# The last expert's first layer reads its rows, or writes its bank, in interleaved orders of columns

## The chip, the cores and the metric

The kernel runs on one core of one Trainium2 chip. The metric is the device time of one execution in microseconds. Five engines work side by side: TensorE (PE, with its weight loads apart as PEld), VectorE (DVE), ScalarE (ACT), GpSimd (POOL) and SyncE (SP), which issues most transfers. SBUF is the memory that the engines read; PSUM holds matmul results, in banks of 512 float32 values per partition.

## What is computed

The first half is a retention layer: for every batch and head a state decays by a factor and takes in one outer product of key and value at each step, and the query reads it. Its result, 3072 rows of 512 values, goes through a mixture of eight experts of which each row uses one:

```python
logits = x @ w_gate
expert_idx = np.argmax(logits, axis=1)
...
for e in range(E):
    mask = expert_idx == e
    xe = x[mask]
    h = np.maximum(xe @ w1[e], 0.0)
    ye = h @ w2[e]
    out[mask] = gate_w[mask, None] * ye
```

w1 of an expert is 512 x 1024, w2 is 1024 x 512. Only the first layer, `h`, of one expert is touched by the change.

## The kernel before

The retention part takes the first third of the time: it makes the rows, chooses experts, and scatters the rows into regions of HBM by expert. Then the experts run one after another in a loop over `e` (in `moe_main`); the experts are sorted by their number of rows, and each place in that order has a fixed capacity, `CAPS = [128, 452, 424, 412, 400, 392, 360, 376]`. The last one, `e` = 7, has room for 376 rows.

An expert's rows lie turned in SBUF: `xs[e]` is a pair of tiles of 128 partitions x 4 slices (`kd`) x 452 columns, a column for each row of the expert. Every float32 operand is cut into a high and a low part (`xh` and `xl`, `whi` and `wlo`), and three products of parts stand for one product.

The first layer runs over eight blocks of features, `f` = 0 to 7. A block is 128 features, the partitions of one PSUM bank; the bank's columns are the expert's rows. It takes twelve matmuls (three products times four `kd`) into the bank `ph`, line 1193, and three banks go round. How many columns each matmul takes is set at run time: `columns` (line 986) compares the number of rows that the expert holds with three widths, for the last expert 360, 368 and 376, and branches to a copy of the twelve matmuls of that width. When a block is done, ScalarE takes the bank through a Relu into `hh` (line 1200, the high part) and VectorE subtracts to get `hl` (line 1201); both always cover the whole capacity, `cap`. After each block some small jobs follow, such as cutting weights (lines 147 and 148) and scattering results of the expert before (line 860 on GpSimd).

The second layer reads `hh` and `hl` of all eight blocks. For the last expert its rows come as the result's partitions, in three steps of up to 128 rows: line 1223 for two steps, and line 1041 for the last one, in two halves of 256 result columns, whose `rhs` is read in runs of 64 columns. Within a step the blocks are taken in order, three matmuls each. The result goes through VectorE (lines 1024 and 1047) and a scatter on GpSimd (line 860) to the output.

The order of the work is that of the code: the schedule is manual, each engine runs its instructions in the order written, and waits by semaphores.

Some other lines come up below. Line 410 sums logits in PSUM over four parts that lie 32 columns apart. Line 826 reads the 7 x 7 table `sel` turned, so each value is 7 values (28 bytes) behind the last, and line 798 reads the same table in order. Line 470 reads a bf16 table at steps of 8 values (16 bytes). Line 465 sums over a row in order. Line 501 writes single values into `xrow` at steps of 130 values (520 bytes).

## Time and profile before

| what | value |
|---|---|
| median of 3 runs | 379.49 us (379.46 to 383.19) |
| the profiled execution | 379.21 us |
| its span, first to last instruction | 377.4 us |
| TensorE busy | 370.0 us (98% of the span) |
| VectorE, ScalarE, GpSimd busy | 255.1, 140.6, 261.7 us |
| mean granted TensorE clock | 1.000 |

The profile is taken from one execution. Its times count from the first instruction. A busy TensorE is one that has a matmul in its pipeline: matmuls overlap, so a matmul's duration is longer than the time from its start to the next one's start, and it is starts that say how fast the stream goes.

## The change

For the last expert alone (`COMBED` = 7) a table gives each of the eight blocks an order of columns: `b` parts, runs of `c` columns, and whether the reading of x (`read`) or the writing of the bank (`write`) is interleaved. A reading with b = 2, c = 1 takes column 0, 188, 1, 189 and so on; one with b = 188, c = 1 takes every second column, then the others; with b = 2, c = 4 it takes four columns of the first half, four of the second, and so on. A writing with c = 4 or 2 puts runs of four or two alternately into the two halves of the bank's 376 columns. All twelve matmuls of a block use the same order. The evictions put the columns back into their natural order, so `hh` and `hl` and all behind them are as before; where c is above 1 an eviction is split into `b` = 2 pieces of 188 columns. The expert no longer branches by its number of rows: it always takes 376 columns.

```diff
+COMBED = 7
+COMBS = ((1, 1, 0, 0), (2, 1, 1, 0), (2, 4, 0, 1), (4, 1, 1, 0), (2, 2, 0, 1), (8, 1, 1, 0), (2, 4, 1, 0), (188, 1, 1, 0))
...
+                b, c, read, write = COMBS[f] if e == COMBED else (1, 1, 0, 0)
+                comb = lambda t, apart: (
+                    t if b == 1 else t.rearrange("p (b a c) -> p a b c" if apart else "p (a b c) -> p a b c", b=b, c=c))
...
-                            nc.tensor.matmul(out=ph[:, :w], lhsT=wparts[e, f // 4][a][:, kd, fo:fo + P],
-                                             rhs=x[:, kd, :w], start=(n == 0), stop=(n == 3 * KD - 1))
+                            nc.tensor.matmul(out=comb(ph[:, :w], write), lhsT=wparts[e, f // 4][a][:, kd, fo:fo + P],
+                                             rhs=comb(x[:, kd, :w], read), start=(n == 0), stop=(n == 3 * KD - 1))
...
-                columns(e, hidden)
+                if e == COMBED:
+                    hidden(cap)
+                else:
+                    columns(e, hidden)
...
-                nc.scalar.activation(out=hh[:, :cap], in_=ph[:, :cap], func=AF.Relu)
-                nc.vector.scalar_tensor_tensor(out=hl[:, :cap], in0=ph[:, :cap], scalar=0.0,
-                                               in1=hh[:, :cap].bitcast(F32), op0=ALU.max, op1=ALU.subtract)
+                piece = lambda t, apart, i: (comb(t, apart) if c == 1 else t.rearrange(
+                    "p (b a c) -> p b a c" if apart else "p (a b c) -> p b a c", b=b, c=c)[:, i])
+                for i in range(b if c > 1 else 1):
+                    hhi, hli, phi = [piece(t[:, :cap], apart, i) for t, apart in ((hh, read), (hl, read), (ph, write))]
+                    nc.scalar.activation(out=hhi, in_=phi, func=AF.Relu)
+                    nc.vector.scalar_tensor_tensor(out=hli, in0=phi, scalar=0.0, in1=hhi.bitcast(F32),
+                                                   op0=ALU.max, op1=ALU.subtract)
```

On TensorE, at the start of the last expert's first layer, there stood before, for block 0 (bank `ph_2198`), the three widths behind two branches:

```order
L986 COMPARE_AND_BRANCH
L1193 MATMUL ph_2198<-xh,whi 128x360 x4
L1193 MATMUL ph_2198<-xh,wlo 128x360 x4
L1193 MATMUL ph_2198<-xl,whi 128x360 x4
L986 UNCONDITIONAL_BRANCH
L986 COMPARE_AND_BRANCH
L1193 MATMUL ph_2198<-xh,whi 128x368 x4
L1193 MATMUL ph_2198<-xh,wlo 128x368 x4
L1193 MATMUL ph_2198<-xl,whi 128x368 x4
L986 UNCONDITIONAL_BRANCH
L1193 MATMUL ph_2198<-xh,whi 128x376 x4
```

In the changed kernel (line 1193 is 1199 there) there stand blocks 1, 2, 3 and 4 one behind the other, without a branch; the shape shown is that of the bank's side:

```order
L1199 MATMUL ph_2199<-xh,whi 128x376 x4
L1199 MATMUL ph_2199<-xh,wlo 128x376 x4
L1199 MATMUL ph_2199<-xl,whi 128x376 x4
L1199 MATMUL ph_2197<-xh,whi 128x47x2x4 x4
L1199 MATMUL ph_2197<-xh,wlo 128x47x2x4 x4
L1199 MATMUL ph_2197<-xl,whi 128x47x2x4 x4
L1199 MATMUL ph_2198<-xh,whi 128x376 x4
L1199 MATMUL ph_2198<-xh,wlo 128x376 x4
L1199 MATMUL ph_2198<-xl,whi 128x376 x4
L1199 MATMUL ph_2199<-xh,whi 128x94x2x2 x4
L1199 MATMUL ph_2199<-xh,wlo 128x94x2x2 x4
L1199 MATMUL ph_2199<-xl,whi 128x94x2x2 x4
```

The number of matmuls is the same, twelve a block; their width and the order of their columns are new. On ScalarE the same stretch read before, from the eviction of block 0 on (in brackets the semaphores, by the engine that raises them, that an instruction waits for):

```order
L1200 ACTIVATE hh<-ph_2198 128x376 [waits PE_49,Activation_49]
L147 CAST whi<-raw 128x1024 [waits DMAHW2_49,Activation_49]
L986 UNCONDITIONAL_BRANCH
L1200 ACTIVATE hh<-ph_2199 128x376 [waits PE_49,Activation_49]
L147 CAST whi<-raw 128x1024
L1200 ACTIVATE hh<-ph_2197 128x376 [waits PE_49,Activation_49]
```

and after, from the eviction of block 1 to that of block 7:

```order
L1213 ACTIVATE hh<-ph_2199 128x188x2 [waits PE_49,Activation_49]
L149 CAST whi<-raw 128x1024
L1213 ACTIVATE hh<-ph_2197 128x47x4 [waits PE_49,Activation_49]
L1213 ACTIVATE hh<-ph_2197 128x47x4 [waits DVE_49]
L1213 ACTIVATE hh<-ph_2198 128x94x4 [waits PE_49,Activation_49]
L1213 ACTIVATE hh<-ph_2199 128x94x2 [waits PE_49,Activation_49]
L1213 ACTIVATE hh<-ph_2199 128x94x2 [waits DVE_49]
L1213 ACTIVATE hh<-ph_2197 128x47x8 [waits PE_49,Activation_49]
L1213 ACTIVATE hh<-ph_2198 128x188 [waits PE_49,Activation_49]
L1213 ACTIVATE hh<-ph_2198 128x188 [waits DVE_49]
L1213 ACTIVATE hh<-ph_2199 128x2x188 [waits PE_49,Activation_49]
```

Blocks 2, 4 and 6 have two evictions, the second of which waits for VectorE. VectorE's side, line 1214 there, is cut in the same way. GpSimd's and SyncE's instructions keep their order.

## Rows read from the trace of the kernel before

**Rows 1.** The page: busy us (share of the span) and instructions of each engine.

```profile
PE 370.0 (98%) x3279; PEld 348.4 (92%) x3279; DVE 255.1 (68%) x499; ACT 140.6 (37%) x252; POOL 261.7 (69%) x277
```

**Rows 2.** Busy time by stage: stretch, its us, each engine's busy us, clock, DMA.

```profile
339.37:355.20 15.83, 15.83 (x98) 15.83 (x97) 8.60 (x13) 5.26 (x9) 12.86 (x14) 1.00 0.09 28
355.20:372.00 16.80, 16.80 (x97) 14.62 (x96) 2.53 (x4) 0.48 (x1) 12.23 (x15) 1.00 0.17 55
```

**Rows 3.** Who waited for whom from 338 us on: total us, times, longest.

```profile
ACT hh L1200 <- PE ph L1193: 12.6, 8, 4.0
DVE yo L1024 <- PE py L1223: 9.3, 2, 4.8
```

**Rows 4.** GpSimd's timeline at the end: start, us, what, idle before and its releaser.

```profile
372.98 1.01 POOL L860 DMA_INDIRECT out<-yo,pair  x1 [1.80 <-DVE yo L1047]
```

**Rows 5.** TensorE's timeline, last expert's first layer, four matmuls a row.

```profile
339.37 0.82 PE L1193 MATMUL ph<-xh,whi 128*128 128x360 f32 x4
340.03 0.82 PE L1193 MATMUL ph<-xh,wlo 128*128 128x360 f32 x4
```

**Rows 6.** The same of an expert with 392 columns, five blocks apart.

```profile
240.10 0.88 PE L1193 MATMUL ph<-xh,whi 128*128 128x392 f32 x4
...
250.80 0.52 PE L1193 MATMUL ph<-xh,whi 128*128 128x392 f32 x2
```

**Rows 7.** TensorE's timeline, last second layer: 512 columns, then runs of 64.

```profile
355.20 0.40 PE L1223 MATMUL py<-whi,hh 128*128 128x512 f32 x1
...
356.83 0.40 PE L1223 MATMUL py<-wlo,hh 128*128 128x512 f32 x1
...
366.33 0.28 PE L1041 MATMUL py<-whi,hh 128*120 128x256 f32 x1
...
367.51 0.28 PE L1041 MATMUL py<-wlo,hh 128*120 128x256 f32 x1
```

**Rows 8.** Groups by shape: count | busy us, mean ns of one | idle before.

```profile
L1200 ACT ACTIVATE hh<-ph 128x452 fp32r<-128x452 f32 x8 | 4.4, 548 | 9.1 <-PE ph L1193 9.0
L1200 ACT ACTIVATE hh<-ph 128x376 fp32r<-128x376 f32 x8 | 3.9, 486 | 12.6 <-PE ph L1193 12.6
L501 ACT COPY xrow<-GW 128x8 f32<-128x8 f32 x4 | 0.8, 205 | 6.0 <-DVE GW L496 6.0
L501 ACT COPY xrow<-GW 128x24 f32<-128x24 f32 x2 | 0.5, 239 | 5.1 <-DVE GW L496 5.1
L1201 DVE SCALAR_TENSOR_TENSOR hl<-ph,hh 128x452 fp32r<-128x452 f32 x8 | 5.0, 625 | 2.7 <-ACT hh L1200 2.1
L1201 DVE SCALAR_TENSOR_TENSOR hl<-ph,hh 128x376 fp32r<-128x376 f32 x8 | 4.4, 547 | 7.1 <-ACT hh L1200 7.0
L410 DVE TENSOR_REDUCE lg<-lp 128x16 f32<-128x64 f32 x8 | 1.8, 223 | 6.7 <-PE lp L404 6.7
L465 DVE TENSOR_REDUCE KEY<-rk 128x2 int32<-128x16 f32 x4 | 0.7, 170 | 0.1
L470 DVE TENSOR_REDUCE tot<-EA 128x8 bf16<-128x16 bf16 x3 | 0.5, 151 | 0.0
L465 DVE TENSOR_REDUCE KEY<-rk 128x6 int32<-128x48 f32 x2 | 0.4, 203 | 0.1
L470 DVE TENSOR_REDUCE tot<-EA 128x8 bf16<-128x48 bf16 x2 | 0.4, 200 | 0.0
L826 DVE TENSOR_TENSOR se<-sel,cs 128x49 f32<-128x49 f32 x1 | 0.3, 252 | 0.0
L798 DVE TENSOR_TENSOR se<-sel,others 128x49 f32<-128x49 f32 x1 | 0.2, 202 | 0.0
```

**Rows 9.** Evictions of the last expert: timelines of ScalarE and VectorE.

```profile
341.61 0.49 ACT L1200 ACTIVATE hh<-ph 128x376 fp32r<-128x376 f32 x1 [4.05 <-PE ph L1193]
342.13 0.55 DVE L1201 SCALAR_TENSOR_TENSOR hl<-ph,hh 128x376 fp32r<-128x376 f32 x1
355.92 0.55 DVE L1201 SCALAR_TENSOR_TENSOR hl<-ph,hh 128x376 fp32r<-128x376 f32 x1 [1.43 <-ACT hh L1200]
```

## What I expected of the change before it ran

> **What bounds the kernel now.** I read the page first. TensorE is busy 370.0 of 377.4 us [rows 1]. So whatever lengthens TensorE's stream lengthens the run, if the engine is not waiting there. The table by stage says where the change lies: the last expert's first layer runs from 339.37 to 355.20, 15.83 us with TensorE busy for 15.83 of them and a clock of 1.00, and the last second layer follows without a gap, 16.80 of 16.80 us [rows 2]. TensorE is not among the waiters of that stretch: the longest waits are ScalarE's for a bank from TensorE (12.6 us) and VectorE's for TensorE (9.3 us) [rows 3]. Behind TensorE's last matmul only one VectorE step, one GpSimd scatter and its landing are left: GpSimd waited 1.80 us for VectorE before the last scatter at 372.98 [rows 4]. So a microsecond more on TensorE between 339 and 355 is a microsecond more in the time.

> The profiled execution took 379.21 us with a span of 377.4; the sum below is made on 379.21, which is 0.28 under the median of 379.49.

> **The change part by part.**

> *No arms any more.* Before, each block takes the narrowest of 360, 368 and 376 columns that holds the expert's rows, and every matmul of the trace took 360 [rows 5]; after, all 96 take 376. A block of twelve lasts 15.83/8 = 1.979 us at 360 columns [rows 2]. At 392 columns five blocks run from 240.10 to 250.80, 10.70/5 = 2.140 us [rows 6]. That is 0.161 us for 32 columns, so 0.080 for 16: a block of 376 takes 2.059 us, and eight cost 8 x 0.080 = **0.64 us**. The branch that goes away gives nothing back: 1.979 us over twelve is 165 ns a matmul, and four matmuls of one kind within a block take 0.66 us, 165 ns too [rows 5].

> *Reads of x in another order.* Blocks 1, 3 and 5 read x one column at a time from 2, 4 or 8 places of the row, so neighbours in the stream lie 752, 376 or 188 bytes apart. Block 6 takes runs of four columns (16 bytes) from two places, block 7 every second column (8 bytes apart). No TensorE row of before steps through its moving operand by single columns. The nearest, the last rows' matmuls, jump after each run of 64 columns: ten of them from 366.33 to 367.51, 118 ns for 256 columns, 0.46 ns each, against (356.83 - 355.20)/7 = 233 ns for 512 in a row, also 0.46 [rows 7]. So a jump as such is free, and the lower bound for all five blocks is nothing (a gain is excluded: no matmul streams fewer columns). The upper bound comes from other engines that step through SBUF element by element. VectorE's product of 49 values reads `sel` in order in 202 ns (L798), and turned, at 28 bytes a step, in 252 (L826): 50 ns more over 49 values, 1.0 ns each, and a value in order costs (203 - 170)/32 = 1.03 ns (L465): the price doubles. At 16 bytes a step (L470) it is (200 - 151)/32 = 1.53 ns, half as much again. ScalarE's writes at 520 bytes a step (L501) cost (239 - 205)/16 = 2.1 ns, against (548 - 486)/76 = 0.82 in order (L1200) [rows 8]. Three rows of two engines say that single four-byte elements, each far from the last, run at half rate or a little worse. I take half rate for TensorE in blocks 1, 3 and 5: each goes from 2.059 to 4.118 us, 3 x 2.059 = **6.18 us**. For runs of four (block 6) I take the row of jumps, nothing. For steps of 8 bytes (block 7) I take nothing too, since that lies nearer to stepping by 4 than to the 16 bytes that cost half; its bounds are 0 and 2.06 us.

> *Writes of the bank in another order.* Blocks 2 and 4 write runs of four and of two columns alternately into the two halves. No row shows TensorE writing so. VectorE's sum of 64 logits reads PSUM at 128 bytes a step in 223 ns (L410); at 1.03 ns a value from the 170 ns of 16 values (L465) 64 in order would be 219 [rows 8]. So a PSUM walk with gaps costs VectorE nothing, and I take 0 for TensorE's; the other bound is half rate, 2 x 2.059 = 4.12 us. [...]

> *Evictions.* They are as wide as before (376) and now step; those of blocks 2, 4 and 6 come in two pieces of 188, where ScalarE's second waits for VectorE's first, by the order above. Now one takes 486 ns on ScalarE and 547 on VectorE [rows 8]. The chain of block 0 runs from 341.61 to 342.13 + 0.55 = 342.68 [rows 9], and its bank is written again by block 3, at 339.37 + 3 x 1.979 = 345.31: 2.6 us of cover. Two pieces cost two more fixed parts: at 0.82 and (625 - 547)/76 = 1.03 ns a value, 188 take 332 and 353 ns, so two of each in series take 1.37 us against 1.03. A stepped eviction of block 1 at the dearest price of rows 8 takes 486 + 376 x 1.3 = 0.97 us on ScalarE and 547 + 376 x 1.0 = 0.92 on VectorE: 0.9 us more. Both stay under the cover, which grows as blocks get longer. Behind block 7 the second layer needs its result only at its 22nd matmul, 21 x 0.233 = 4.9 us on, and it is ready 1.3 us after the layer's end now [rows 7, 9]. So **0**; without that cover each of the seven would cost up to 0.9 us.

> *The tail.* GpSimd waits for VectorE, and VectorE for TensorE, before the last scatter [rows 3, 4]; a later TensorE moves them along: 0.

> Sum: 379.21 + 0.64 + 6.18 = **386.0 us**, 1.7% above the median.

> **The rivals.**

> *Stepped reads are free on TensorE.* Then only the columns are left: 379.21 + 0.64 = 379.9 us, not slower. [...] Against it: three rows that agree in direction. It decides if a block of 1, 3, 5 costs less than 1.1 us extra, for then the sum stays under 1% (383.3). A half price, as at 16 bytes (1.03 us a block), gives 382.9 and falls here.

> *Writes into the bank in runs are slow as well:* 386.0 + 4.12 = 390.1 us. For it nothing in a row; against it L410. [...] If only they are slow, 384.0.

> *Stepping by 8 bytes is slow as well:* 386.0 + 2.06 = 388.1 us.

> *TensorE pays the other engines' nanoseconds, not their ratio.* At 1.0 ns more for each of 376 columns, 36 matmuls pay 13.5 us: 379.85 + 13.5 = 393.4. For it: VectorE's and ScalarE's stepped prices, 2.1 ns, are alike though their rates in order differ. I hold it less likely, since TensorE takes 0.46 ns a column now, so it reads faster than either.

> *The evictions become the bound:* TensorE would show waits for a bank at blocks 3 to 7. The cover of 2.6 us against 0.9 speaks against it; chance next to nothing.

> **How the numbers follow.** Half rate in three blocks alone 0.43 (own range 385.0 to 386.6: the doubling taken as 0.95 to 1.05); free 0.24 and half price 0.08; with PSUM writes 0.13, of which 0.02 without the reads; with the 8-byte steps 0.06; the nanoseconds 0.06. The time forecast is the likeliest one's, 386.0. From 379.6 (free, less the 0.3 that executions differ) to 390.4 all is held but the last: about 0.9, and it could not end lower without leaving out a bound that no row closes. About 1% is what a measurement of this kernel can tell from no change. Slower by more: 0.43 + 0.13 + 0.06 + 0.06 = 0.68; within: 0.31; faster: 0.01, for nothing in the change shortens TensorE's stream.

> **What would show it.** In the changed profile the last first layer should last 15.83 + 6.82 = 22.7 us. The starts of TensorE's groups of four say which step was right: 0.69 us from group to group in blocks 0, 2, 4, 6 and 7, and 1.37 in blocks 1, 3 and 5. 0.69 everywhere makes the first rival right; 1.37 in blocks 2 and 4 the second, in block 7 the third; over 2 in blocks 1, 3, 5 the fourth. TensorE gaps before blocks 3 to 7 with ScalarE or VectorE as their end would show the evictions. The prediction is wrong above all if the moving operand goes through a path that does not care where the next column lies, or if 2, 4 and 8 places differ, which I have not priced.

## The result, and the profile of the changed kernel

| what | before | changed |
|---|---|---|
| median of 16 runs each | 379.48 us | 384.05 us |
| ratio, 95% interval | | 1.012 (1.0096 to 1.0144) |
| the last first layer on TensorE | 15.83 us [rows 2] | 20.58 us |
| the last second layer, to TensorE's end | 16.95 us | 16.98 us |

The changed kernel is slower by 4.6 us, a little over 1%; forecast were 386.0 us. A ratio leaves out the slowed-down executions, which the medians keep, so it is not exactly the quotient of two medians. The execution that was profiled first (388.28 us) lost 4.3 us ahead of the change, about places where TensorE was idle (0.58 us before 23.93, 1.90 before 98.17). The times of its other runs (at most 385.79) and a second profile of the same kernel do not show that loss, so all rows of the changed kernel are from the second profile (384.33 us, span 382.5). It reaches the layer at 339.64, where before it was 339.37 [rows 5].

The page's engines, as [rows 1]: TensorE has 5.0 us more, the others at most 1.8.

```profile
PE 375.0 (98%) x3279; PEld 349.9 (91%) x3279; DVE 256.9 (67%) x502; ACT 142.2 (37%) x255; POOL 260.6 (68%) x277
```

The two stages, as [rows 2], with the same columns (stretch, its length, then the engines' busy time, clock, DMA share and GB/s):

```profile
339.64:360.22 20.58, 20.58 (x98) 17.51 (x97) 10.14 (x16) 6.88 (x12) 15.64 (x19) 1.00 0.10 30
360.22:377.20 16.98, 16.98 (x97) 14.63 (x95) 2.53 (x4) 0.52 (x1) 8.00 (x10) 1.00 0.14 45
```

TensorE is busy in every microsecond of both, at a granted clock of 1.00: the 4.75 us are longer matmuls and no wait. Where they lie is read from starts. This is TensorE's timeline, as [rows 5] (start, us, what), with the first group of each of the eight blocks, the second group of block 0, and the first matmul of the second layer:

```profile
339.64 0.85 PE L1199 MATMUL ph<-xh,whi 128*128 128x376 f32 x4
340.33 0.85 PE L1199 MATMUL ph<-xh,wlo 128*128 128x376 f32 x4
...
341.70 0.80 PE L1199 MATMUL ph<-xh,whi 128*128 128x376 f32 x4
...
343.61 0.85 PE L1199 MATMUL ph<-xh,whi 128*128 128x376 f32 x4
...
345.68 0.96 PE L1199 MATMUL ph<-xh,whi 128*128 128x376 f32 x4
...
348.08 0.86 PE L1199 MATMUL ph<-xh,whi 128*128 128x376 f32 x4
...
350.15 1.47 PE L1199 MATMUL ph<-xh,whi 128*128 128x376 f32 x4
...
354.04 0.90 PE L1199 MATMUL ph<-xh,whi 128*128 128x376 f32 x4
...
356.23 1.50 PE L1199 MATMUL ph<-xh,whi 128*128 128x376 f32 x4
...
360.22 0.41 PE L1236 MATMUL py<-whi,hh 128*128 128x512 f32 x1
```

The difference of two starts is a block, and a twelfth of it a matmul:

| block | order | us | ns a matmul | forecast us |
|---|---|---|---|---|
| 0 | as it was | 2.06 | 172 | 2.06 |
| 1 | reads two places | 1.91 | 159 | 4.12 |
| 2 | writes runs of four | 2.07 | 172 | 2.06 |
| 3 | reads four places | 2.40 | 200 | 4.12 |
| 4 | writes runs of two | 2.07 | 172 | 2.06 |
| 5 | reads eight places | 3.89 | 324 | 4.12 |
| 6 | reads runs of four, two places | 2.19 | 182 | 2.06 |
| 7 | reads every second column | 3.99 | 332 | 2.06 |

The reads alone differ: two places are *faster* than columns in a row (159 ns against 172), four a little slower, eight nearly twice as slow, and so is every second column. Here more places also lie closer together; which of the two counts, the measuring kernels below tell apart.

The waits of that stretch, from 338 us on, as [rows 3] (total, times, longest):

```profile
ACT hh L1213 <- PE ph L1199: 14.0, 8, 4.1
...
POOL out L862 <- DVE yo L1049: 3.4, 2, 1.8
...
ACT hh L1213 <- DVE hl L1214: 1.7, 3, 0.9
```

No row has TensorE as the waiter. The new one, ScalarE for VectorE, three times, is the second pieces of blocks 2, 4 and 6. GpSimd's last wait is 1.8 us as in [rows 4], so the tail is what it was. The evictions, as [rows 9], on ScalarE in blocks 0, 1, 2 (two pieces), 5 and 7, and on VectorE in blocks 1 and 7:

```profile
341.96 0.48 ACT L1213 ACTIVATE hh<-ph 128x376 fp32r<-128x376 f32 x1 [4.13 <-PE ph L1199]
343.87 0.88 ACT L1213 ACTIVATE hh<-ph 128x376 fp32r<-128x376 f32 x1 [0.49 <-PE ph L1199]
345.94 0.33 ACT L1213 ACTIVATE hh<-ph 128x188 fp32r<-128x188 f32 x1 [0.33 <-PE ph L1199]
347.16 0.33 ACT L1213 ACTIVATE hh<-ph 128x188 fp32r<-128x188 f32 x1 [0.90 <-DVE hl L1214]
354.32 0.85 ACT L1213 ACTIVATE hh<-ph 128x376 fp32r<-128x376 f32 x1 [2.78 <-PE ph L1199]
360.50 0.52 ACT L1213 ACTIVATE hh<-ph 128x376 fp32r<-128x376 f32 x1 [2.93 <-PE ph L1199]
```

```profile
344.79 0.86 DVE L1214 SCALAR_TENSOR_TENSOR hl<-ph,hh 128x376 fp32r<-128x376 f32 x1
...
361.05 0.55 DVE L1214 SCALAR_TENSOR_TENSOR hl<-ph,hh 128x376 fp32r<-128x376 f32 x1 [3.10 <-ACT hh L1213]
```

ScalarE, which reads the bank in order and writes `hh` at the interleaved places, takes 1.8 times as long for single columns at far places (0.88 us for 0.48). VectorE, which reads `hh` and writes `hl` there, takes 1.6 times as long (0.86 for 0.55). Two places or eight are alike, and every second column costs next to nothing (0.52 and 0.55). TensorE's order is another: it pays for the second column (332 ns a matmul for 172) and not for the two places (159).

## The experiments

Every kernel was run beside runs of the kernel before on the same chip, and a ratio is to those.

### The changed kernel again

No edit; it asks whether the loss ahead of the change belongs to it.

> The changed kernel once more, unedited, beside runs of before on the same chip. Its first profile lost 4.3 us ahead of the change, at 22 and 95 us. If that has nothing to do with the change, a second profile reaches the last expert's first layer near 339.3, as before did, spends 20.6 us in it again, and the time is about 384.0; if it belongs to the change, the loss comes back.

Measured: 383.95 us against 379.03, ratio 1.012 (1.0086 to 1.0153). The early loss was gone (the layer begins at 339.64, in the first profile at 343.66); the layer itself lasted 20.58 us in both profiles. So nothing shows the early loss to be the change's.

### The columns alone

```diff
-COMBS = ((1, 1, 0, 0), (2, 1, 1, 0), (2, 4, 0, 1), (4, 1, 1, 0), (2, 2, 0, 1), (8, 1, 1, 0), (2, 4, 1, 0), (188, 1, 1, 0))
+COMBS = ((1, 1, 0, 0),) * 8
```

> All eight blocks of the last expert read and write their columns in the natural order, at 376 columns and without the branches: the term of the wider matmuls alone. By the prediction's first term (blocks of 2.059 us instead of 1.979) the last first layer lasts 16.47 us and the time is 0.64 us over before, about 380.1 against 379.5. Rival: the missing branches give something back, so no difference or faster.

Measured: 379.97 us against 379.25, ratio 1.0024 (1.0013 to 1.0036). TensorE's timeline, blocks 0 and 1 and the start of the second layer:

```profile
339.23 0.85 PE L1199 MATMUL ph<-xh,whi 128*128 128x376 f32 x4
...
341.29 0.86 PE L1199 MATMUL ph<-xh,whi 128*128 128x376 f32 x4
...
355.80 0.40 PE L1236 MATMUL py<-whi,hh 128*128 128x512 f32 x1
```

The layer takes 16.57 us, 0.74 more than before, and a block 2.071. The first term of the sum (0.64) is right, and every order below is measured against 2.07.

### Without the orders of blocks 5 and 7

```diff
-COMBS = (..., (2, 2, 0, 1), (8, 1, 1, 0), (2, 4, 1, 0), (188, 1, 1, 0))
+COMBS = (..., (2, 2, 0, 1), (1, 1, 0, 0), (2, 4, 1, 0), (1, 1, 0, 0))
```

> As changed, but blocks 5 (eight places) and 7 (every second column) in the natural order. In the changed kernel's trace blocks 5 and 7 took 3.9 and 4.0 us where 2.06 is natural, block 3 2.41, block 6 2.19 and block 1 only 1.91. Theory 'two blocks pay': the time falls by (3.9 - 2.06) + (4.0 - 2.06) = 3.8 us, from 384.05 to about 380.3, and the blocks left keep their times. Rival, 'something else in the changed code pays too' (evictions in pieces, waits): less falls away, 381 or more.

Measured: 380.13 us against 379.25, ratio 1.0036 (1.002 to 1.0052). The starts of blocks 0 to 4 in TensorE's timeline, and that of the second layer:

```profile
339.17 0.85 PE L1199 MATMUL ph<-xh,whi 128*128 128x376 f32 x4
...
341.23 0.80 PE L1199 MATMUL ph<-xh,whi 128*128 128x376 f32 x4
...
343.14 0.85 PE L1199 MATMUL ph<-xh,whi 128*128 128x376 f32 x4
...
345.20 0.96 PE L1199 MATMUL ph<-xh,whi 128*128 128x376 f32 x4
...
347.61 0.86 PE L1199 MATMUL ph<-xh,whi 128*128 128x376 f32 x4
...
355.97 0.40 PE L1236 MATMUL py<-whi,hh 128*128 128x512 f32 x1
```

Again 1.91, 2.06 and 2.41 us for blocks 1, 2 and 3, and the layer takes 16.80 us, 0.23 more than with the columns alone. So blocks 5 and 7 carry 20.58 - 16.80 = 3.78 of the 4.75 us, and each block pays for its own order.

### Two places in all eight blocks

```diff
-COMBS = ((1, 1, 0, 0), (2, 1, 1, 0), (2, 4, 0, 1), ...)
+COMBS = ((2, 1, 1, 0),) * 8
```

> All eight blocks read in block 1's order, alternately from two places 752 bytes apart; evictions step accordingly. Theory 'two places are faster than a row in order': 1.91 us a block, 15.3 us for the layer, against 16.47 in the natural order at 376 columns, so 1.2 us less than that: about 379.0, 0.5 under before although each matmul has 16 columns more. Rival 'block 1 was only faster by its place in the program': 2.06 us a block, 380.1. Rival 'the stepped evictions (0.88 and 0.86 us a block in the changed trace) become the bound': TensorE waits before blocks 3 to 7, over 380.1.

Measured: 378.70 us against 379.25, ratio 0.999 (0.9959 to 1.0022), and in TensorE's timeline:

```profile
339.28 0.80 PE L1199 MATMUL ph<-xh,whi 128*128 128x376 f32 x4
...
354.56 0.39 PE L1236 MATMUL py<-whi,hh 128*128 128x512 f32 x1
```

The layer takes 15.28 us, 1.91 a block. It streams 376 columns in less time than the kernel before streams 360 (15.83). So the gain of block 1 is no accident of its place; whether the whole is faster than before the interval leaves open. All eight evictions took 0.84 to 0.88 us on ScalarE, and TensorE did not wait in that stretch.

### Measuring kernels: orders of 320 columns

Two kernels stream 320 columns (256 or 128 in some) of a tile of weights through eleven matmuls in each of 56 blocks, every block in another order; the first matmul of a block stays as it was. What they leave out: the first layers of experts 1 to 7 are not computed, so their time (390.61 and 380.77 us) says nothing. `walk` builds the order from nested steps and counts:

```diff
+def walk(t, dims):
...
+    at, *dims = dims
+    v = bass.AP(t.tensor, t.offset + at, [list(t.ap[0])] + [[step, count] for step, count in dims])
+    return v
...
+                            if n:
+                                o = walk(ph, bank_dims)
+                                r = walk(wparts[e, f // 4][a].rearrange("p k f -> p (k f)"), flat)
```

> A measuring kernel: in the first layers of experts 1 to 7 (56 blocks) the first matmul of a block is natural, and the other eleven read 320 columns of a weights tile (2048 columns in a row) in an order of their own, so what is computed there is not the layer; each expert always takes its capacity. Steps of 1 to 6 columns, two places 1 to 1024 columns apart, four, eight, ten and sixteen places, runs of 2 and 4, one column again and again, and writes in runs. In order 320 columns should take 0.449 x 320 = 144 to 146 ns. Theory 'places' (what counts is in how many places the reading stands at once, and whether both columns of an 8-byte pair are used before they are dropped): every step of 2 or more takes 0.87 x 320 = 277 ns; two places 136 ns at any distance; eight places 277 ns at any distance; runs of two columns near 146 ns from any number of places. Theory 'distance' (what counts is how far a column lies from the one before: 752 bytes free, 376 a quarter, 188 and 8 bytes all): two places 47 columns apart take 277 ns, 94 apart 171, 188 apart 136; eight places 188 apart 136 ns; steps differ among each other. Writes in runs of two: 146 ns by both.

The first kernel's timeline of TensorE, pairs of neighbouring groups: in order, every second column, two places 188 columns apart, four places 94 apart, runs of two from two places:

```profile
132.40 0.75 PE L1271 MATMUL ph<-wlo 128*128 128x320 f32 x4
132.99 0.31 PE L1271 MATMUL ph<-whi 128*128 128x320 f32 x1
...
135.62 1.03 PE L1271 MATMUL ph<-whi 128*128 128x320 f32 x3
136.48 1.31 PE L1271 MATMUL ph<-wlo 128*128 128x320 f32 x4
...
217.48 0.71 PE L1271 MATMUL ph<-wlo 128*128 128x320 f32 x4
218.03 0.57 PE L1271 MATMUL ph<-whi 128*128 128x320 f32 x3
...
244.21 0.86 PE L1271 MATMUL ph<-wlo 128*128 128x320 f32 x4
244.89 0.69 PE L1271 MATMUL ph<-whi 128*128 128x320 f32 x3
...
323.03 1.00 PE L1271 MATMUL ph<-wlo 128*128 128x320 f32 x4
323.86 0.81 PE L1271 MATMUL ph<-whi 128*128 128x320 f32 x3
```

From start to start that is 0.59/4 = 147 ns, 0.86/3 = 287, 0.55/4 = 137, 0.68/4 = 170 and 0.83/4 = 207 ns a matmul. The medians over the eleven of each block:

```
320 columns                                         ns a matmul
in order, from column 0 / from column 1             147 / 149
steps of 2, 3, 4, 5, 6                              284, 283, 290, 287, 280
two places, 1 to 1024 columns apart (19 distances)  135 to 137
four places, 47 apart                               147
four places, 64 to 512 apart (7 even distances)     171 to 177
eight places (8 distances), ten, sixteen            273 to 300
runs of two, from two places / from eight           209 / 293
runs of four, from two places / from eight          153 / 153
one column all the time                             138
writes in runs of two (three patterns)              146, 146, 147
runs of two, read from two places and written so    215
```

Between two places the distance does not matter, down to a single column (135 to 137 ns), and the number of places does (171 to 177 ns at four and even distances, 273 to 300 from eight on). Writes in runs of two are free where the reading is in order (146 and 147 ns for 147); together with reads in runs of two they took 215 ns for 209. The odd one is four places at 47, which costs nothing (147 ns) where 64, 94 and 96 do (171 to 177).

One way of counting fits most of it, within some 6%: call it the **two halves**. It is an estimate, worked out from these medians. The columns at even and at odd positions of the stream are counted apart, as two halves, and the tile is counted in pieces of four columns (16 bytes), a length with which it agrees that runs of four from two places cost 153 ns and runs of two 209. A step of a half is a new piece if its column lies in none of the last two or three pieces that the half read from. A pair of columns is put at 0.85 ns (136/160); a new piece at 0.92 ns more if the step before or after it in the same half is a new piece too, and at 0.14 if not ((147 - 136)/80, from the row in order). With steps of 2 every step of a half is a new piece: 160 x (0.85 + 0.92) = 283 (the row from which the 0.92 is taken). From two places each half walks one place in order, a new piece at every fourth step: 136 + 40 x 0.14 = 142, a little over the 136 measured. From four places a half alternates between two, and meets their new pieces one behind the other if they begin at the same column of a piece, which an even distance makes so (places of one half lie two distances apart), and at different times if the distance is odd, as 47 is. The second kernel tries this: odd against even distances, runs that don't begin with a piece, orders within four and eight columns.

> Measured as before: eleven of twelve matmuls of each first-layer block read 320 columns (or the number named) of a weights tile in an order of their own, so what is computed there is not the layer. Theory 'two halves', made from the first measuring kernel: the columns at even and at odd positions of the stream are served apart, each half from lines of 16 bytes (four columns); a half that stays on a line or moves on after two or more columns costs little, but where one change of line follows another each costs some 0.92 ns. It says: four places an even number of columns apart 171 to 177 ns (both places of a half change line together), an odd number apart 136 to 147 (they change in turn); two places in which the reading steps by 2 columns 147 ns or less, though a plain step of 2 took 284; by 4 columns 283; runs of two from two places about 209 at any distance; the order 0, 4, 1, 5 within eight columns 136, 0, 2, 1, 3 within four about 147, 0, 2, 4, 6, 1, 3 within eight near 284; six places 0.87 ns a column if a half holds two lines, 0.6 if three. Rival theory 'places' (the number of places alone counts, and steps of more than one column take half rate): four places 173 at any distance, two places with steps of 2 columns 283, 0, 2, 1, 3 like a plain row.

The medians, beside what that count gives:

```
320 columns                                         measured    counted
four places, 8 even distances (44 to 190)           170 to 173  173 to 175
four places, 8 odd distances (45 to 191)            144 to 147  143 to 144
two places, each in steps of 2                      141 to 151  147 to 149
two places, each in steps of 4                      283, 284    283
two places, each in steps of 3                      213         246
runs of two, from two places (4 distances)          206 to 209  210
runs of four, two places, not aligned (4 distances) 207         209
runs of eight, from two places / from eight         153 / 147   147
backwards / pairs turned / 0 2 1 3                  147/146/147 147
0 4 1 5 2 6 3 7                                     136         142
0 2 4 6 1 3 5 7                                     213         210
six places, 318 columns (odd and even distances)    187         174 even, 144 odd
256 columns: in order                               120         118
256 columns: two places / four, 256 apart           112 / 143   113 / 138
256 columns: steps of 2                             228         227
128 columns: the same four orders                   111 to 116  (57 to 113)
```

Odd against even came out in 16 of 16 distances. Two rows miss the count: steps of 3 from two places come cheaper, and six places dearer, without a difference between odd and even (with two pieces kept by a half they count to 281, so the count needs three at least in part; 0.6 ns a column, expected for that case, comes to 191). A third row missed what I expected: `0 2 4 6 1 3 5 7`, put near 284, counts to 210 once a half is allowed more than one piece. The expectation on runs of four that are not aligned I had not made; the count of 209 is made afterwards. At 128 columns the order no longer matters (111 to 116 ns in all four), so something else than the order sets that time. Only the first interval of each of these four blocks, right behind a matmul of 376 columns, still goes by the order (57, 55, 69 and 94 ns). The weight loads, one for each matmul, start as far apart there (in order, four from 350.75 to 351.20); whether they are the limit was not tried.

### All matmuls from two places

If two places are faster than a row, a kernel that *stores* rows apart gains in all layers that stream them. Row r of an expert goes to column 226 (r mod 2) + r/2 of `xh` and `xl`, and the same for `hh` and `hl` of experts 1 to 6; the casts and evictions that write them step through their input by 8 bytes, and the matmuls of these layers read columns 0, 226, 1, 227 and so on, so that the bank comes out in natural order. The branches by width stay.

```diff
+def both(x, w):
+    return x.rearrange("p (b a) -> p a b", b=2)[:, 0:w // 2]
...
-            cut_high(nc, xs[e][0], *args)
+            apart_high(nc, xs[e][0], *args)
...
-                                             rhs=x[:, kd, :w], start=(n == 0), stop=(n == 3 * KD - 1))
+                                             rhs=both(x[:, kd], w), start=(n == 0), stop=(n == 3 * KD - 1))
...
+                if e not in natural:
+                    hhv, hlv = [t.rearrange("p (b a) -> p b a", b=2)[:, :, 0:cap // 2] for t in (hh, hl)]
+                    phv = phv.rearrange("p (a b) -> p b a", b=2)
...
-                                                 rhs=x[:, :c], **se)
+                                                 rhs=both(x, c), **se)
```

> The kernel before, with its branches, in which all moving rows of experts 1 to 7 lie apart: row r of an expert at column 226 (r mod 2) + r / 2 of xh and xl, and in experts 1 to 6 of hh and hl, put there by the casts and evictions that write them anyway; every matmul of the first layers and of the second layers of experts 1 to 6 then reads from two places in turn and gives its columns in the natural order. Nothing is left out. Theory 'two places are faster than a row in order' (159 against 172 ns for 376 columns): 11.5 to 14.5 ns less for each of 1248 matmuls, 16.1 us, so about 363.2 us. Rival 'TensorE is no longer the bound then' (GpSimd's scatters, VectorE's splits or the weights' transfers make it wait): less than 10 us, 370 or more. Rival 'the casts and evictions that step by 8 bytes cost VectorE and ScalarE what TensorE gains': no gain, 379.

Measured: 367.44 us against 379.17, ratio 0.9675 (0.9638 to 0.9713): faster than both kernels, by 11.7 us where 16.1 were expected. It was run again, beside a version of which only the first layers read two places (`hh` and `hl` and the second layers as before):

> The kernel that reads all moving rows from two places, unedited, for a second profile: 16.1 us were worked out, 11.7 came. In the first profile TensorE stood idle for 3.8 us between 156 and 196 us and the last scatter was some 1.1 us later behind TensorE's end than before. If these are what is missing, the second profile shows them again, at the same places; if they were that execution's own, its span is some 4 us shorter than 365.6.

> As the kernel that reads all moving rows from two places, but for the first layers alone (672 matmuls); the second layers read in order, and the evictions are those of before. Theory 'what the other engines let through is limited': of 8.6 us that the matmuls save, nearly all arrives, about 370.8, since TensorE still is the slower one. Rival 'the casts that lie apart cost elsewhere': clearly less than half, 375 or more.

Measured: 366.73 us against 379.03, ratio 0.9667 (0.9623 to 0.9711), and for the first layers alone 372.78 us, ratio 0.9839 (0.9776 to 0.9901). So the first layers alone give 6.3 us of 8.6 expected (their matmuls save 8.5, counted from start to start), and all together 12.3 of 16.1. The page's engines of the full version, and TensorE's timeline: the last first layer at 360 columns, TensorE's last matmul, that of the kernel before, and the three places after 100 us at which TensorE was idle in the full version (idle us and releaser in brackets):

```profile
PE 356.0 (97%) x3279; PEld 333.9 (91%) x3279; DVE 252.7 (69%) x499; ACT 141.1 (39%) x252; POOL 263.4 (72%) x277
```

```profile
330.98 0.77 PE L1210 MATMUL ph<-xh,whi 128*128 128x360 f32 x4
331.59 0.77 PE L1210 MATMUL ph<-xh,wlo 128*128 128x360 f32 x4
...
358.63 0.28 PE L1058 MATMUL py<-whi,hl 128*120 128x256 f32 x1
```

```profile
371.88 0.28 PE L1041 MATMUL py<-whi,hl 128*120 128x256 f32 x1
```

```profile
153.59 0.44 PE L1246 MATMUL py<-hh,whi 128*128 128x420 f32 x1 [0.32 <-issue]
181.85 0.97 PE L1210 MATMUL ph<-xh,whi 128*128 128x416 f32 x4 [0.46 <-DVE hl L1222]
189.77 0.43 PE L1246 MATMUL py<-hh,whi 128*128 128x416 f32 x1 [1.07 <-issue]
```

A matmul of 360 columns takes 0.61/4 = 153 ns where it took 165 [rows 5], 0.42 ns a column. TensorE's last matmul starts at 358.63 for 371.88 before: 13.2 us earlier. Counted from start to start, the 1248 matmuls themselves give 15.8 of the 16.1 us. Some 2.6 us are lost again about the idle places (1.85 us of idle time, the rest slower starts beside them). These places are new: in the kernel before TensorE waits for nothing behind 7.9 us. And the end is 1.1 us longer (span less TensorE's end, 6.4 for 5.3). The first profile of this version had both too, with 3.8 us of idle time in the same stretch. What is late now, the waits of ScalarE (the full version, then the kernel before), the cutting of weights on ScalarE and VectorE ahead of 181.85, and the tail on VectorE and GpSimd say:

```profile
ACT whi L147 <- DMA raw<-w: 11.7, 6, 3.4
```

```profile
ACT whi L147 <- DMA raw<-w: 2.8, 4, 1.0
```

```profile
178.99 1.04 ACT L147 CAST whi<-raw 128x1024 fp32r<-128x1024 f32 x1 [3.36 <-DMA raw<-w]
```

```profile
180.06 1.22 DVE L148 TENSOR_TENSOR wlo<-raw,whi 128x1024 fp32r<-128x1024 f32 x1 [3.80 <-ACT whi L147]
```

```profile
358.75 0.88 DVE L1064 TENSOR_SCALAR yo<-py,meta 120x256 f32<-120x256 f32 x2 [4.70 <-DMA out<-yo,sidx]
```

```profile
355.87 1.01 POOL L860 DMA_INDIRECT out<-yo,sidx  x1 [0.16 <-issue]
...
357.68 1.01 POOL L860 DMA_INDIRECT out<-yo,sidx  x1 [0.16 <-issue]
```

ScalarE waits 11.7 us for weights to land before it cuts them, where it was 2.8, and GpSimd scatters the last second layer's first rows only at 355.87 and 357.68, behind other scatters (0.16 us of idle between them), so VectorE gets a buffer for the last rows at 358.75. With TensorE shorter, the transfers of weights and GpSimd's queue begin to end last. The idle place at 181.85 can be followed back in the trace: ScalarE waits 3.36 us for weights, VectorE 3.80 for ScalarE, VectorE's eviction `hl` comes behind that, and TensorE waits for it. The place at 153.59 comes behind a wait for weights too (1.69 us, at 149.63 on ScalarE); just ahead of the one at 189.77 there is none, so its cause stays open. No run here tried earlier weights.

## Why the prediction was right in size and wrong in its steps

**The place and the cover were right.** The layer is TensorE's alone, and the whole of its 4.75 us reached the end (TensorE's last matmul ends at 377.20 for 372.16: 0.27 from a later start of the layer, 4.75, and 0.03), and the tail cost nothing.

**No arms: right**, 0.74 measured for 0.64.

**Blocks 1, 3 and 5 at half rate: this step failed.** I priced them at 2.06 us each, 6.18 in all; against 2.07 they took -0.16, +0.33 and +1.82, 1.99 in all. Near half rate holds for eight places only. What failed is the carrying over: rows 8 show VectorE and ScalarE stepping, and those engines indeed pay for block 1, 1.8 and 1.6 times (0.88 and 0.86 us), while TensorE, reading the very same interleave, is faster than in order (159 ns for 172). The carrying was weak in two more ways: ScalarE's row is one of writes, and of the three rows of "single four-byte elements" L470 reads two-byte values (bf16). My sentence on the jumps, "a gain is excluded: no matmul streams fewer columns", was wrong as well: columns in order are not the fastest stream. And "2, 4 and 8 places differ, which I have not priced" was the condition under which I said it would fail.

**Block 7 free: this step failed too.** It cost 1.92 us, near its upper bound of 2.06. I chose by the nearest step length in rows of VectorE, where 8 bytes are close to 4; on TensorE steps of 2 columns cost the same as steps of 6 (284 and 280 ns).

**Block 6** took 0.12 us more than in order instead of nothing; counting by halves gives it nothing either, so this stays open (the measuring kernels have it too, 153 for 147).

**Writes free: right.** Blocks 2 and 4 took 2.07 us, as in order, and three scattered patterns of writes that keep pairs together took 146, 146 and 147 ns against 147. No run shows the 4.12 us of the rival that such writes cost as much again; no run breaks a pair.

**Evictions free: right**, with the prices near what I bounded (0.88 and 0.86 for at most 0.97 and 0.92; pieces of 0.33 and 0.35 as worked out), and TensorE did not wait.

The size came out by luck. The sum, 6.82 us, came within 2.1 us of the 4.75 because two errors of opposite sign met: 4.2 us too much for blocks 1, 3 and 5, and 1.9 too little for block 7. Of the steps that make it slower only block 5's held, and that alone, 1.82 us or 0.5%, would have stayed under my 1%; block 7, which I had at nothing, brings it over. Without both the kernel is 0.4% slower. The time also lies below the range that I gave to half rate itself (385.0 to 386.6; by the factors named its lower end is 385.4), and close to the 384.0 that I gave for slow writes alone, which the starts of blocks 2 and 4 refute. No rival as priced describes all five blocks of reads: free reads hold for block 1 alone, the price of 8-byte steps for block 7, a half price and the nanoseconds of other engines for none.

**What stands in their place.** The orders in the kernel agree with the count by halves at 188 pairs: block 3, 204 ns counted for 200 measured; block 5, 333 for 324; block 7, 333 for 332; block 1, 166 for 159. In the count a half takes two columns from a piece before it moves on in order (147 ns for 320 columns), four from two places (135 to 137), one at every second column (284). Counted over the whole stream, with one piece held at a time, two places would be as slow as eight, which they are not (135 to 137 ns against 273 to 300). The two halves are a count that fits the measured orders; what in the chip makes them, no run shows.

## What to carry to other kernels

Where TensorE is the bound, let matmuls of float32 parts (here of type fp32r) read their moving operand alternately from two places: 0.42 ns a column for 0.46 in order, at every distance tried from 1 to 1024 columns, and 3.3% of this whole kernel. Don't step through a row by two to six columns (280 to 290 ns for 320 columns against 147 in order), and don't alternate between eight places (273 to 300), which nearly doubles its time. A price of one engine's access pattern need not hold for another, nor a write's for a read: in the same interleave TensorE reads at -8%, VectorE reads and writes at +56%, and ScalarE writes at +83%.
